# Order inside a step of seven matmul pairs: the dense lane's maximum product first, the other lane e m e m e e m

## The chip, the cores and the metric

The kernel runs on one NeuronCore of a Trainium2 chip. Its time is the device time of one execution in microseconds (us); lower is better. The engines that matter here are TensorE (PE in the profile; its weight loads are PEld), VectorE (DVE), ScalarE (ACT), GpSimd (POOL) and SyncE (SP), which issues the DMAs.

## The reference

A layernorm of x (2048 tokens of width 512) feeds two branches: attention with 32 query heads of width 16 that share one key and one value head, and a dense layer of width 1792 with Mish. The second gates the first.

```python
x = A_x
xn = _layernorm(x, axis=-1)
# A: q = xn @ wq in 32 heads, k = xn @ wk, v = xn @ wv
scores = jnp.einsum("bhqd,bkd->bhqk", q, k) * (Dh ** -0.5)
p = _softmax(scores, axis=-1)
o = jnp.einsum("bhqk,bkd->bhqd", p, v)
s = o.transpose(0, 2, 1, 3).reshape(B, S, H * Dh) @ wo
# B: h = xn @ w1 + b1, act = h * tanh(softplus(h))
g = _silu(act @ w2)
return x + s * g
```

Inputs and outputs are float32. The matmuls of this kernel split each operand into a high and a low part and add three products.

## The kernel before

The attention runs over 32 blocks (4 chunks of 512 queries, 8 groups of 4 heads in each), and a block is 16 steps. `s` counts the steps, and a step treats 2 x 2 score tiles. In one step TensorE makes, for the main part of the kernel:

- four **e** products (`e_one`): scores, keys on the partitions, 128 x 512. ScalarE turns each into its exponential `pt` (line L910). They use three PSUM banks in turn.
- four **m** products (`m_one`): scores of a later block, queries on the partitions, of which VectorE takes the row maximum (line L932). They too have three PSUM banks. From these maxima `c_rows` makes the shift rows of a block (lines L951 to L961, once per block), on VectorE as well.
- four **pv** products: values times the exponentials of two steps before. The trace shows each as two matmuls, so eight.
- six, seven, eight or no **x** products: halves of the other matmuls (q projection, dense layers 1 and 2, output projection). Such a matmul group has 12 or 15 products, all into the one PSUM bank `xps`; its sum is then read out (evacuated) by ScalarE (`hb` of the first dense layer, `qf` of the queries, `y` of the second layer's first third) or by VectorE (later thirds, `y` line L745, and the gate).

The e, m and x products use 64 of the array's 128 rows each, so that two run at once, one in either half. A half is called a lane here. In step s the **dense lane** is s % 2: the x products run there. The **other lane** has the four e and n of the m products; the remaining 4 - n are the dense lane's. `m_sides` sets n from the number k of x products: n is 3 for six and seven of them, 4 for eight. With six, both lanes have seven products, and the step is seven pairs; I call it a six-step, and those with seven and eight x a seven-step and an eight-step. A group of 12 takes four six-steps: six products in one lane, the same six (other half of the rows) in the other lane, then again. A group of 15 takes two eight-steps and two seven-steps.

`waves` writes the pairs out, an x and then one product of the other lane, until both lists are empty. The order on all engines is the order in which the code is written; nothing is reordered by a scheduler. Three rules in `waves` matter:

- **The relay.** The two halves of a product add into one bank from different lanes. So the first x of a step waits for an instruction of the step before: the consumer (exponential or maximum) of the first product that the other lane gets once the step's x products are all issued.
- **The evacuation** is issued right behind the last x of a group (`finish`), ahead of whatever the code issues later on that engine.
- **The hold.** If VectorE evacuates, the maxima issued while only one x is left (`HOLD`) go behind the evacuation.

Before, the other lane's list is made from the pattern "MEMEMEME", in which an M is left out when there is none: with n = 3 it is m e m e m e e.

Of the kernel before, what the change touches and what calls it, by code (L numbers as in the profile page):

```python
# [43 lines left out]
STEP_US = 2.95  # L44
XMAX = 8
NPT = 14
EM = "MEMEMEME"
MLAG = 4
NHB = 4
NXR = 2  # L50
# [12 lines left out]
def m_need(v):  # L63

    return (34, 64)[v] if v < 2 else 32 * (v + 1)
# [53 lines left out]
def block_kernel(ctx: ExitStack, tc: tile.TileContext, x, wq, wk, wv, wo, w1, b1, w2, out):  # L119
# [349 lines left out]

    held = [None]  # L470
    evacs = [0]
    cur = {"g": None, "ps": None, "n": 0, "chunk": [], "relay": None}

    def is_ready(g):
        return (all(i.tile is not None and i.ready <= step[0] for i in g.items)
# [7 lines left out]
    def begin():  # L483
        prepare()
        if qqueue and is_ready(qqueue[0]):
            g = qqueue.popleft()
        elif queue and is_ready(queue[0]):
            g = queue.popleft()
        else:
            n = next((n for n, g in enumerate(queue) if g.wo is None), None)  # L490
            if not n or not is_ready(queue[n]) or queue[n].m1 is None:
                return False
            g = queue[n]
            del queue[n]
        if g.start:
            g.start()
        if g.alloc:
            ps = g.alloc()
        else:
            ps = ps_x.tile([P, 512], F32, tag="x", name="xps")  # L500
        cur.update(g=g, n=0, ps=ps, chunk=[], relay=None)
        return True

    def finish():
        g = cur["g"]
        if cur["n"] < len(g.mms):
            return False
        for i in g.items:
            i.users -= 1
        cur["g"] = None  # L510
        evacs[0] += g.dve
        if lead:
            lead["post"](g, cur["ps"])
        else:
            g.post(cur["ps"])
            g.done = step[0]
        return True
# [14 lines left out]
    def chunk_size(n):  # L532
        return -(-n // -(-n // XMAX)) if n else 0

    def waves(h, em, new):

        if not cur["chunk"] and (not new or cur["g"] is None and not begin()):  # L540
            mms = []
        else:
            g = cur["g"]
            mms = cur["chunk"] or g.mms[cur["n"]:cur["n"] + chunk_size(len(g.mms) - cur["n"])]
        second = bool(cur["chunk"])
        k = len(mms)
        ms = em(k)
        a = deque(ms[1 - h])
        b = deque(ms[h])
        ps = cur["ps"]  # L550
        ends = second and cur["n"] + k == len(cur["g"].mms)
        xs = deque(mms)
        relay = None
        first = True
        done = False
        while a or b or xs:
            if xs:
                i = xs.popleft().half(ps, h)
                if first and cur["relay"] is not None:
                    tc.add_manual_dep(i.ins, cur["relay"].ins.name, mybir.DependencyInfo(  # L560
                        mybir.DependencyClass.Sync, mybir.DependencyReason.DATA), reason="other half of the bank")
                first = False
                if ends and cur["g"].dve and len(xs) == HOLD:
                    held[0] = []
                if not xs and ends:
                    cur["n"] += k
                    cur["chunk"] = []
                    finish()
                    done = True
                    for top in held[0] or ():  # L570
                        top()
                    held[0] = None
            elif b:
                b.popleft()()
            if len(a) > 1 or a and not xs:
                r = a.popleft()()
                if k and not xs and relay is None:
                    relay = r
        if k and not done:
            assert relay is not None  # L580
            cur["relay"] = relay
            if second:
                cur["n"] += k
                cur["chunk"] = []
            else:
                cur["chunk"] = mms
# [310 lines left out]
    def e_one(s, i):  # L897

        v, r = divmod(s, 16)
        if s < NS - LEAD:  # L900
            a, k, p = 1 - s % 2, r - r % 2 + i // 2, i % 2
        else:
            a, k, p = i % 2, r, i // 2
        q = qt_of[v]
        o = 64 * a
        ps, tag = (ps_m, "m") if NS - LEAD <= s and i in ((1, 3) if s < NS - 4 else (3,)) else (ps_e, "e")
        e = ps.tile([P, C], F32, tag=tag, name=f"e{s}_{i}")
        pe.matmul(e, ks[o:o + 64, P * k:P * (k + 1)], q[o:o + 64, p], start=True, stop=True)  # L908
        pt = sb.tile([P, C], F32, tag="pt", name=f"pt{s}_{i}", bufs=NPT)
        r = act.activation(pt, e, AF.Exp, scale=0.25)  # L910
        pt_of[16 * v + k, p, a] = pt
        return r
# [24 lines left out]
    def m_sides(h, n):  # L937

        ahead = m_next[h] - m_next[1 - h]
        lo = max((4 - MLAG - ahead + 1) // 2, 4 - (32 * NU - m_next[1 - h]))  # L940
        hi = min((4 + MLAG - ahead) // 2, 32 * NU - m_next[h])
        return max(min(n, hi), lo)
# [116 lines left out]
    def due(t):  # L1059
        step[0] = t  # L1060
        for k in sorted(k for k in timed if k <= t):
            for fn in timed.pop(k):
                fn()
# [84 lines left out]
    for c0, c1 in ((0, 1), (1, 2), (2, 3), (3, 4)):  # L1148
# [4 lines left out]
        for c in range(c0, c1):  # L1153
            xs, scs = [], []
# [65 lines left out]
    def best(eng):  # L1220
        found = None
        for k in plan[eng]:
            s = k.start(T[eng])
            if s is not None:
                rank = max(s, T[eng] + 0.1) + WAIT_US * k.prio
                if found is None or rank < found[2]:
                    found = (s, k, rank)
        return found
# [5 lines left out]
    while True:  # L1234
# [7 lines left out]
        b = best("PE")  # L1242
# [13 lines left out]
        s, e, k = min(opts, key=lambda o: o[0])  # L1256
# [34 lines left out]
        elif k == "J":  # L1291
            tag = next((g for g in ("wq", "ws", "wb") if (g == "wq" or s > 19.0) and arrived(g) and busy[0] + E0 < s + 0.5), None)
            n = ran[0]
# [16 lines left out]
    while left:  # L1310
        k = next(k for k in left if all(d.end is not None for d in k.deps))
# [10 lines left out]
    def pv_to(s):  # L1322

        while pv_next[0] <= s:
            k = pv_next[0]
            pv(k)
            pv_next[0] += 1
            if k % 16 == 15:
                o_out(k // 16)
                return  # L1330

    for s in range(NS + 2000):
        inm = s < NS - LEAD
        if inm or cur["chunk"]:
            assert s < NS
            due(s)
            h = s % 2

            def em(k):
                n = m_sides(1 - h, k // 2) if inm else 0  # L1340
                x = deque(lambda i=i: e_one(s, i) for i in range(4))
                y = deque(lambda: m_one(1 - h) for _ in range(n))
                r = [[], []]
                for op in EM:
                    if op == "M" and y:
                        r[1 - h].append(y.popleft())
                    elif op == "E":
                        r[1 - h].append(x.popleft())
                r[h] = [lambda: m_one(h) for _ in range(4 - n if inm else 0)]
                return r  # L1350

            if s >= 2 and (s - 1) % 16 == 0 and s > 1:
                gap[0] += 1
            waves(h, em, inm)
            act_jobs(1 + (len(jobs) > 2))
            due(s + 0.5)
            pv_to(s - 2)
            last = s + 1
        elif s < NS:
            if s == last and (NS - s) % 2:  # L1360
                for k in range(4):
                    e_one(s, k)
                due(s)
                fill(4)
                act_jobs(1)
                pv_to(s - 2)
            elif (NS - s) % 2 == 0:
                for k in range(6):
                    e_one(s + k // 4, k % 4)
                due(s)  # L1370
                fill(4)
                act_jobs(1)
            else:
                for k in range(2, 4):
                    e_one(s, k)
                due(s)
                fill(4)
                act_jobs(2)
                pv_to(s - 1)
        else:  # L1380
            due(s)
            act_jobs(100)
            pv_to(NS - 1)
            due(s + 0.5)
            fill(16)
        step[0] = s
        if vdone[0] < 8 * NC and min(m_next) >= m_need(vdone[0]):
            r = c_rows(vdone[0])
            rowq.extend([r[0], lambda r=r: (r[1](), r[2](), r[3]())])
            vdone[0] += 1  # L1390
        if rowq and not evacs[0]:
            rowq.popleft()()
        evacs[0] = 0
        pump()
        if s > NS + 1 and not queue and cur["g"] is None and not timed and not jobs:
            break
# [12 lines left out]
```

## Time and profile before

| | before |
|---|---|
| time, median of 3 runs | 1607.55 us (1606.56 to 1608.75) |
| span of the profiled execution | 1607.2 us |
| TensorE matmul busy | 1590.6 us (99%) |
| TensorE weight loads busy | 847.8 us (53%) |
| VectorE busy | 1344.9 us (84%) |
| ScalarE busy | 1298.3 us (81%) |
| GpSimd busy | 625.4 us (39%) |

The profiled execution's time is its span; the median of the runs is 0.3 us above it. TensorE's share is the time in which any matmul is under way, and since matmuls overlap and their ends are modelled, 99% doesn't mean that it could do no more.

### The profile page before, as it was taken

Reading aid. Unit: us, or ns where it says so; the run is one execution under the profiler, and the core shown is the slowest. Engines: PE = TensorE matmul, PEld = TensorE weight load, DVE = VectorE, ACT = ScalarE, POOL = GpSimd, SP = SyncE. Lnnn points to the kernel's source line nnn. Section 1 sums busy time; section 2 is a strip of 40 time slices with the busy share of each in tenths; the row PEclk is TensorE's granted clock in tenths of the full one; section 3 lists DMA queues with packets and bytes.
Section 4 is the critical chain, followed back from the end, with each engine's and each line's share of the span. In section 5 each row is a group of like instructions: output and inputs, shape, how many; then the busy total and the mean of one; then the engine's idle time right before and its main releaser. Section 6 shows DMA issues by size and latency. Waiting matters only on the chain.

```text
span 1607.2 us, 31497 instructions
## 1 busy us (share of the span) xinstructions
PE 1590.6 (99%) x11611; PEld 847.8 (53%) x11611; DVE 1344.9 (84%) x2299; ACT 1298.3 (81%) x2512; POOL 625.4 (39%) x640
## 2 busy tenths in 40 slices
PE   9999999999999999999999999999999999999998
PEld 5445555555555555555555555555555555555544
DVE  8898888888888888888898988888888888888812
ACT  7478788688898778978988787787798878779885
POOL 3276278066355103612514322172152323315522
PEclk9899999999999999999999999999999999999999
DMA  6233133142321304212103231221331223022020
GB/s 192 72 116 96 51 108 115 29 149 83 101 90 38 111 16 140 64 48 88 39 24 109 64 116 44 87 71 35 96 109 58 83 61 97 24 96 70 8 86 27
DMA packets 73001, 125.08 MB, mean 78 GB/s; under 512 B 21520, under 2 KB 33808, under 8 KB 72848
## 3 DMA queue, kind: packets, MB, share of 16 engines
q1 hardware_dynamic: 72848, 123.08, 24.4%
q8 instruction: 92, 1.51, 0.4%
q14 instruction: 61, 0.50, 0.1%
HBM read 75.57 MB, written 26.21 MB: 63 GB/s over the span
## 4 chain that ended last, share of the span: by engine, by line
PE 96%; DVE 1%; ACT 1%; POOL 0%; DMA 0%; SPq 0%; issue 0%; DVEq 0%; POOLq 0%
PE xps L112 43%; PE pv L982 32%; PE e L908 9%; PE m L928 8%; PE xps L108 3%; PE kp L312 1%; DVE mb L932 1%; PE wop L108 1%; ACT pt L910 0%; PE xp L280 0%; DMA xin<-in_dram 0%; DVE xt L156 0%; SPq L217 0%; ACT hb L671 0%; PE ol L1045 0%
## 5 line engine op out<-in xcount | busy, mean ns | idle before, releaser
L932 DVE TENSOR_REDUCE mb<-m 128x1 f32<-128x512 f32 x2048 | 1271.2, 682 | 184.2 <-PE m L928 149.0
L910 ACT ACTIVATE pt<-e 128x512 f32<-128x512 f32 x2048 | 1068.2, 605 | 250.9 <-PE e L908 240.9
L928 PE MATMUL m<-ks,qt 48*128 48x512 f32 (+1 forms) x2048 | 845.8, 424 | 4.2 <-DVE mb L932 2.9
L908 PE MATMUL e<-qt,ks 64*128 64x512 f32 x2048 | 746.7, 408 | 2.4 <-ACT pt L910 1.6
L982 PE MATMUL pv<-pt,vaug 128*32 128x512 f32 x4096 | 543.1, 604 | 0.0
L928 PEld LDWEIGHTS m<-ks,qt 48*128 48x128 f32 (+1 forms) x2048 | 373.1, 186 | 76.3 <-DVE mb L932 38.0
L908 PEld LDWEIGHTS e<-qt,ks 64*128 64x128 f32 x2048 | 372.4, 186 | 26.2 <-ACT pt L910 11.1
L112 PE MATMUL xps<-xt,ws 64*128 64x512 f32 x1266 | 351.2, 409 | 0.9 <-ACT pt L910 0.4
L112 PEld LDWEIGHTS xps<-xt,ws 64*128 64x128 f32 x1266 | 218.0, 185 | 204.8 <-ACT pt L910 137.7
L112 PE MATMUL xps<-wbs,act 64*128 64x512 f32 x1188 | 321.3, 407 | 0.0
L112 PEld LDWEIGHTS xps<-wbs,act 64*128 64x128 f32 x1188 | 207.0, 185 | 168.7 <-ACT pt L910 103.9
L166 POOL TENSOR_SCALAR t<-t 128x512 f32<-128x512 f32 x56 | 34.4, 614 | 323.8 <-ACT t L679 323.8
L982 PEld LDWEIGHTS pv<-pt,vaug 128*32 128x32 f32 x4096 | 81.9, 108 | 144.1 <-issue 135.8
L156 POOL TENSOR_TENSOR hb<-hb,t 128x512 f32<-128x512 f32 x56 | 72.2, 1289 | 116.1 <-ACT t L692 64.1
L112 PE MATMUL xps<-xt,wq 64*128 64x512 f32 x336 | 93.0, 409 | 0.0
L112 PEld LDWEIGHTS xps<-xt,wq 64*128 64x128 f32 x336 | 57.9, 185 | 54.1 <-ACT pt L910 35.2
L112 PE MATMUL xps<-wbs,ot_all 64*128 64x512 f32 x288 | 79.4, 408 | 0.0
L112 PEld LDWEIGHTS xps<-wbs,ot_all 64*128 64x128 f32 x288 | 49.5, 184 | 46.9 <-ACT pt L910 31.0
L156 POOL TENSOR_TENSOR hb<-hb,u 128x512 f32<-128x512 f32 x56 | 72.2, 1290 | 4.4
L156 POOL TENSOR_TENSOR u<-u,t 128x512 f32<-128x512 f32 x56 | 71.8, 1281 | 4.7
L156 POOL TENSOR_TENSOR act<-hb,act 128x512 fp32r<-128x512 f32 x55 | 70.7, 1286 | 4.6
L156 POOL TENSOR_TENSOR oc<-oc,sc 128x512 f32<-128x512 f32 (+1 forms) x16 | 20.6, 1287 | 121.3 <-ACT sc L1010 110.6
(121 smaller groups left out, 822.4 us busy)
## 6 DMA issues: line engine op xcount, KB each, us to landing
ws<-w SPq DMA_DIRECT2D x38, 512.0 KB
wbs<-w SPq DMA_DIRECT2D x36, 512.0 KB
qt<-qh SPq DMA_DIRECT2D x256, 32.0 KB
wq<-wq SPq DMA_DIRECT2D x14, 512.0 KB
w<-wbs SPq DMA_DIRECT2D x14, 512.0 KB
w<-ws SPq DMA_DIRECT2D x14, 512.0 KB
wbs<-wo SPq DMA_DIRECT2D x12, 512.0 KB
rawwb<-in_dram SPq DMA_DIRECT2D x20, 256.0 KB
```

Source lines behind the costliest of these rows:

```text
L108: self.pe.matmul(ps, self.lhs(), self.rhs(), start=(self.k == 0), stop=(self.k == self.tot - 1))
L112: i = self.pe.matmul(ps, self.lhs()[o], self.rhs()[o], start=(self.k == 0 and self.halves == 0), stop=(self.k == self.tot - 1 and self.hal ...
L156: eng.tensor_tensor(out=o, in0=a, in1=b, op=op)
L166: pool.tensor_scalar(o, o, lim, 0.0, op0=ALU.min, op1=ALU.max)
L312: pe.matmul(kp_of[c], wkf[:, dt], xf_of[c][dt // 2][:, dt % 2], start=(dt == 0), stop=(dt == 3))
L908: pe.matmul(e, ks[o:o + 64, P * k:P * (k + 1)], q[o:o + 64, p], start=True, stop=True)
L910: r = act.activation(pt, e, AF.Exp, scale=0.25)
L928: pe.matmul(m, q[o, p, P * t:P * (t + 1)], ks[o, C * kb:C * (kb + 1)], start=True, stop=True)
L932: return dve.reduce_max(out=mb_of[v][:, kb, z:z + 1], in_=m, axis=AX.X)
L982: pe.matmul(o[32 * j:32 * j + 32], vaug[:, k], pt, start=(k == 0), stop=(k == 15))
```

## The change

The pattern of the other lane depends on n: for three m it becomes e m e m e e m, for four it is as before. And in a step whose other lane has seven products (n is 3) the dense lane's one m is written before the first x, where before it stood behind the last.

```diff
-EM = "MEMEMEME"
+ORDERS = {3: "EMEMEEM", 4: "MEMEMEME"}
...
-    cur = {"g": None, "ps": None, "n": 0, "chunk": [], "relay": None}
+    cur = {"g": None, "ps": None, "n": 0, "chunk": [], "relay": None, "front": False}
...
         ms = em(k)
+        cur["front"] = k > 0 and len(ms[1 - h]) == 7
         a = deque(ms[1 - h])
         b = deque(ms[h])
...
         while a or b or xs:
-            if xs:
+            if xs and b and first and cur["front"]:
+                b.popleft()()
+                cur["front"] = False
+            elif xs:
                 i = xs.popleft().half(ps, h)
...
-                for op in EM:
+                for op in ORDERS.get(n, "MEMEMEME"):
```

The rows below are instructions in program order, with what each waits for in brackets (DVE and Activation are VectorE and ScalarE). First TensorE, the first five products of the step that ends one group of the first dense layer (its x products read `ws`); before:

```order
L112 MATMUL xps<-xt_1811,ws_9147 128x512 [waits Activation_49]
L928 MATMUL m_1_15_9657<-ks,qt_78 128x512 [waits DVE_49]
L112 MATMUL xps<-xt_1811,ws_9147 128x512
L908 MATMUL e_0_9661<-qt_77,ks 128x512
L112 MATMUL xps<-xt_1811,ws_9147 128x512
```

and with the change:

```order
L932 MATMUL m_0_17_9656<-ks,qt_78 128x512 [waits DVE_49]
L912 MATMUL e_0_9659<-qt_77,ks 128x512 [waits Activation_49]
L112 MATMUL xps<-xt_1811,ws_9147 128x512 [waits DVE_49]
L932 MATMUL m_1_15_9664<-ks,qt_78 128x512
L112 MATMUL xps<-xt_1811,ws_9147 128x512
```

The first e moves from the second pair to the first, and the first x from the first pair to the second; that x, the one with the relay, now waits for VectorE and not for ScalarE. The last five products of the same step on TensorE; before:

```order
L928 MATMUL m_1_17_9675<-ks,qt_78 128x512 [waits DVE_49]
L112 MATMUL xps<-xt_1811,ws_9147 128x512
L908 MATMUL e_2_9681<-qt_77,ks 128x512 [waits Activation_49]
L928 MATMUL m_0_17_9685<-ks,qt_78 128x512 [waits DVE_49]
L908 MATMUL e_3_9688<-qt_77,ks 128x512 [waits Activation_49]
```

and with the change:

```order
L912 MATMUL e_2_9677<-qt_77,ks 128x512 [waits Activation_49]
L112 MATMUL xps<-xt_1811,ws_9147 128x512
L912 MATMUL e_3_9682<-qt_77,ks 128x512 [waits Activation_49]
L112 MATMUL xps<-xt_1811,ws_9147 128x512
L932 MATMUL m_1_17_9689<-ks,qt_78 128x512 [waits DVE_49]
```

The fourth e moves from the seventh pair to the sixth, the last x from the sixth to the seventh, and an m is last. ScalarE in this step and at the start of the next; before:

```order
L910 ACTIVATE pt_0_9663<-e_0_9661 128x512 [waits PE_49]
L910 ACTIVATE pt_1_9672<-e_1_9670 128x512 [waits PE_49]
L671 ACTIVATE hb_10_9679<-xps,b1c 128x512 [waits PE_49]
L910 ACTIVATE pt_2_9683<-e_2_9681 128x512 [waits PE_49]
L910 ACTIVATE pt_3_9690<-e_3_9688 128x512 [waits PE_49]
L910 ACTIVATE pt_0_9709<-e_0_9707 128x512 [waits PE_49]
```

and with the change:

```order
L914 ACTIVATE pt_0_9661<-e_0_9659 128x512 [waits PE_49]
L914 ACTIVATE pt_1_9670<-e_1_9668 128x512 [waits PE_49]
L914 ACTIVATE pt_2_9679<-e_2_9677 128x512 [waits PE_49]
L914 ACTIVATE pt_3_9684<-e_3_9682 128x512 [waits PE_49]
L675 ACTIVATE hb_10_9687<-xps,b1c 128x512 [waits PE_49]
L914 ACTIVATE pt_0_9707<-e_0_9705 128x512 [waits PE_49]
```

The evacuation `hb` moves from behind the second exponential to behind the fourth. Of the 512 first exponentials (`pt_0`) of the steps, 236 have a second wait, for ScalarE itself, in the program before, and 34 with the change; of the third ones 77 and 121.

## Rows read from the trace of the kernel before

**Rows 1.** The page: busy time of each engine; the ending chain by line.

```profile
PE 1590.6 (99%) x11611; PEld 847.8 (53%) x11611; DVE 1344.9 (84%) x2299; ACT 1298.3 (81%) x2512; POOL 625.4 (39%) x640
...
PE xps L112 43%; PE pv L982 32%; PE e L908 9%; PE m L928 8%; PE xps L108 3%; PE kp L312 1%; DVE mb L932 1%; PE wop L108 1%; ACT pt L910 0%; PE xp L280 0%; DMA xin<-in_dram 0%; DVE xt L156 0%; SPq L217 0%; ACT hb L671 0%; PE ol L1045 0%
```

**Rows 2.** Groups by line and shape: count | busy us, mean ns | idle before.

```profile
L932 DVE TENSOR_REDUCE mb<-m 128x1 f32<-128x512 f32 x2048 | 1271.2, 682 | 184.2 <-PE m L928 149.0 <-PE xps L112 32.0 <-PE e L908 1.9
L910 ACT ACTIVATE pt<-e 128x512 f32<-128x512 f32 x2048 | 1068.2, 605 | 250.9 <-PE e L908 240.9 <-PE xps L112 3.8 <-PE m L928 1.7
...
L671 ACT ACTIVATE hb<-xps,b1c 128x512 f32<-128x512 f32 x56 | 38.7, 691 | 9.1 <-PE xps L108 9.1
...
L745 DVE TENSOR_TENSOR y<-xps,y 128x512 f32<-128x512 f32 x32 | 21.8, 682 | 51.2 <-PE xps L108 42.9 <-POOL qt L156 8.3
```

**Rows 3.** Busy time by stretch, 318.42 to 550.04: PE, PEld, DVE, ACT, POOL, PEclk.

```profile
318.42:550.04 231.62, 231.62 (x1761) 123.68 (x1761) 205.59 (x349) 197.23 (x380) 114.21 (x116) 1.00 0.30 94
```

**Rows 4.** Timeline of PE, PEld and ACT, six-step from 802.18: start us, us.

```profile
802.18 0.50 PE L112 MATMUL xps<-wbs,act 64*128 64x512 f32 x1
802.52 0.40 PE L908 MATMUL e<-qt,ks 64*128 64x512 f32 x1
803.68 0.49 PE L908 MATMUL e<-qt,ks 64*128 64x512 f32 x1
804.10 1.07 PE L982 MATMUL pv<-pt,vaug 128*32 128x512 f32 x8
805.09 0.50 PE L112 MATMUL xps<-wbs,act 64*128 64x512 f32 x1
...
803.67 0.18 PEld L908 LDWEIGHTS e<-qt,ks 64*128 64x128 f32 x1
...
803.01 2.06 ACT L910 ACTIVATE pt<-e 128x512 f32<-128x512 f32 x4 [0.33 <-PE e L908]
```

**Rows 5.** Timeline of PE, PEld and ACT, six-step from 810.87.

```profile
810.87 0.50 PE L112 MATMUL xps<-wbs,act 64*128 64x512 f32 x1
...
812.29 0.18 PEld L908 LDWEIGHTS e<-qt,ks 64*128 64x128 f32 x1
812.72 0.16 PEld L982 LDWEIGHTS pv<-pt,vaug 128*32 128x32 f32 x8 [0.24 <-issue]
...
811.64 1.57 ACT L910 ACTIVATE pt<-e 128x512 f32<-128x512 f32 x3 [0.27 <-PE e L908]
```

**Rows 6.** Timeline of PE, ACT and DVE, step without x from 98.70.

```profile
98.70 0.49 PE L928 MATMUL m<-ks,qt 64*128 64x512 f32 x1
...
99.27 2.06 ACT L910 ACTIVATE pt<-e 128x512 f32<-128x512 f32 x4
101.19 0.74 ACT L688 ACTIVATE t<-u,two 128x512 f32<-128x512 f32 x1
...
99.23 2.48 DVE L932 TENSOR_REDUCE mb<-m 128x1 f32<-128x512 f32 x4 [0.22 <-PE e L908]
```

**Rows 7.** Timeline of PE, seven-step from 992.35 and the next step's start.

```profile
992.35 0.50 PE L112 MATMUL xps<-wbs,act 64*128 64x512 f32 x1
...
994.09 0.39 PE L928 MATMUL m<-ks,qt 48*128 48x512 f32 x1
994.40 1.07 PE L982 MATMUL pv<-pt,vaug 128*32 128x512 f32 x8
995.40 0.50 PE L112 MATMUL xps<-wbs,act 64*128 64x512 f32 x1
```

**Rows 8.** Timeline of PE, DVE and PEld, six-step behind `c_rows`, from 500.55.

```profile
500.55 0.50 PE L112 MATMUL xps<-wbs,ot_all 64*128 64x512 f32 x1
...
500.86 0.19 DVE L956 TENSOR_REDUCE mp<-mp 128x16 f32<-128x32 f32 x1
...
501.39 1.25 DVE L932 TENSOR_REDUCE mb<-m 128x1 f32<-128x512 f32 x2
...
502.10 0.18 PEld L928 LDWEIGHTS m<-ks,qt 48*128 48x128 f32 x1 [0.31 <-DVE mb L932]
```

## The prediction

> **What bounds the kernel now.** I read the page first: TensorE has a matmul in flight 99% of the span and the chain that ended last runs almost wholly through its lines [rows 1], while VectorE's maxima and ScalarE's exponentials are 84% and 81% busy [rows 1, 2]. A busy TensorE is not a TensorE at its peak, so I went to the timeline of single steps, engine by engine. All times below are microseconds from the first product of a step.
>
> A six-step (six half products x, four e, four m) is one of 360 such steps that I count in the trace; 60 steps have seven x and 60 have eight. Take the one that starts at 802.18 [rows 4]. The products come in pairs, one on each half of the array: the first at 0, the second at 0.34 (802.52), then one every 0.23, so that the seventh stands at 1.50 (803.68). The four e go to pairs 2, 4, 6 and 7. The fourth e takes the PSUM bank of the first e (three banks). The exponential of the first e starts at 0.83 and lasts 0.60 [rows 2, 4]: done at 1.43. The weights of the fourth e are loaded at 1.49 (803.67), 0.06 later, and the pv products begin 0.43 after that load, at 1.92; the next step begins 0.99 after them, at 2.91. In the step at 810.87 the first exponential starts at 0.77 instead, the load comes at 1.42, pv at 1.85: again 0.43 after the load [rows 5]. So in both steps the end is set not by the slots but by one chain: first e, its exponential, the bank, fourth e, pv. The two starts differ because the program gives 236 of the 512 first exponentials a second wait, which costs them 0.06; the step at 810.87 has none.
>
> Without that wait pv could begin some 0.33 behind the seventh pair at 1.505, at 1.84, and a step would last 2.835: in a seven-step, whose last product is an m that waits for nothing, it is 0.31 (994.09 to 994.40 [rows 7]), and the seventh pair has an e a little behind the m. The mean is more: the stretch from 318.42 to 550.04 is 80 six-steps in a row, 231.62 / 80 = 2.895 [rows 3]. There is 0.06 per step to be had, 21.6 in all, and no more while the clock is at 1.00, its upper level of 2.4 GHz, as it is there.
>
> The Trainium skill, page "Perfetto Trace Analysis", section "Identifying the Most-Contended Engine", would judge TensorE by the busy share of its weight loads, not of its matmuls. By that share, 53% [rows 1], TensorE has room and VectorE is the most contended; a step would end no sooner than VectorE's four maxima of 0.60, at 2.4, and not at 2.835. The pairs at 0.23 in rows 4 speak against it: seven pairs and pv alone fill 2.835.
>
> **The change part by part.** No instruction is added or taken away; work is reordered in the 360 six-steps and in the 60 seven-steps, on TensorE, ScalarE and VectorE; the queues of GpSimd and SyncE, and so all DMAs, keep their order.
>
> (1) The first e and the dense lane's m become pair 1. The trace has steps that begin so, those without any x: in the one at 98.70 the first exponential starts at 0.57, the first maximum at 0.53, and the ScalarE instruction behind the four exponentials at 2.49 (101.19) [rows 6]. In the new order the first exponential ends at 1.17 and the fourth e loads at 1.22. It now stands in pair 6 (1.27), not 7; as the matmul follows its load by 0.10 (0.43 less the 0.33 above), it runs at 1.32, 0.05 late. One m follows in its lane, 0.23 later, at 1.55, and pv at 1.88; the step lasts 2.87. So the e that comes 0.34 earlier gives back 0.23 by standing one pair earlier. The gain is 2.895 - 2.87 = 0.025, times 360: **-9.0**. Of the first exponentials 34 keep a second wait in the new program: 34 x 0.06 = **+2.0**.
>
> In a seven-step the m of the other lane stands two pairs behind the fourth e, so nothing is pushed: 3.05 as before [rows 7].
>
> (2) A twelve-product group ends in a six-step, and its sum must leave the single xps bank before the next group's first x. Before, the evacuation stood behind the second exponential and was done long before it was needed. Now the last x is pair 7, and on ScalarE's queue, which runs in order, the evacuation stands behind all four exponentials: it starts at 2.49 and, at 0.69 [rows 2], ends at 3.18. Load at 3.23; the next step began at 2.87, so that is 0.36 into it, and x runs at 0.46. Its slot is now pair 2, at 0.34: 0.12 late, of which the 0.05 that the fourth e is late anyway are free. 52 groups end with hb: 52 x 0.07 = **+3.6**. The 14 copies of q I take at 0.60, like the exponentials, which read a tile of the same size from PSUM: they end 0.09 earlier, and what is left is within the slack: nothing. The 16 copies of y, also at 0.60, end a seven-step at 3.09, load at 3.14; the x that follows is mostly pair 1 of an eight-step, which would begin at 3.05: 16 x 0.09 = **+1.4**.
>
> (3) VectorE's evacuations (y, 0.68 [rows 2]) stood third of five on its queue and now stand fourth: 0.53 + 3 x 0.60 + 0.68 = 3.01, load at 3.06, 0.19 into the next step: in time. But the last maximum then ends at 3.61, its bank is wanted by the next step's pair 4 (2.87 + 0.80) instead of pair 5, and that m runs at 3.76: 0.09 late, 0.045 beyond the slack. 29 six-steps stand behind such a one: **+1.3**.
>
> (4) The half products of a bank change lanes from step to step, and the first x of a step waits for one instruction of the step before, the relay. It was the third exponential, done at 2.4; it becomes the step's last maximum, done at 3.01 (four of them take 2.48 from 0.53 [rows 6]). Load at 3.06, 0.19 into the step; x runs at 0.29, its slot is 0.34. That is free, with 0.05 to spare and 0.05 more behind it. Queued behind this x is everything on TensorE. It isn't free when VectorE has worked on the shift rows (c_rows): there the first maximum starts at 0.84 (501.39 in the step of 500.55), m waits until 1.55 (502.10) and pv, 0.43 behind that load, until 1.98 [rows 8], before and after alike. Now the four maxima also end at 3.29, the relay comes at 3.34 and x at 0.48 of the next step, 0.14 late, 0.09 beyond the slack. Before, the mean of 2.895 has these steps in it; the 2.87 has not, so they are added in full: 24 six-steps x (1.98 - 1.88 + 0.09) = **+4.6**.
>
> The sum is -9.0 + 2.0 + 3.6 + 1.4 + 1.3 + 4.6 = +3.9 on the span of 1607.2, 1611.1. The median of the runs is 0.3 above that span, which is less than the terms can tell: **1611**.
>
> Bounds. The 0.10 from load to matmul is inferred. If a late x must wait until its weights are in (0.18 to 0.19 of load), the waits of (2), (3) and (4) cost 0.09 more each, 121 times: +11, 1622. If the m behind the fourth e isn't pushed, pv comes at 1.84 and all 21.6 are won, but the slack of 0.05 is gone too: hb 52 x 0.155, y 1.4, (3) 29 x 0.125, (4) 24 x 0.27, second waits 1: 20.6 back, 1606.
>
> **The rivals.**
> - *The reorder wins.* The last sentence with the second half going otherwise: the step shrinks to 2.835 and the late evacuations and relays don't bite because VectorE and ScalarE start earlier too. If half of those 20.6 is hidden, 1607.2 - 21.6 + 10.3 = 1596; it is faster than the bound once less than 18 of them remain. For it: the first exponential does come 0.26 earlier. Against it: hb at 3.18 is arithmetic on rows 2 and 6. The share of weight loads in the Trainium skill's page "Perfetto Trace Analysis", named above, would favour this one.
> - *The relay binds every step.* If the wait for the maximum ends 0.1 later than I have it, the 270 six-steps that begin with a relayed x and not a fresh bank lose what goes beyond the slack. From 0.10 on each further 0.05 costs 13; at 0.15 it is 1624.
> - *Nothing measurable.* Gain and costs of some 9 and 13 are of one size; an error of a third in either leaves the time within 3 of now.
>
> **How the numbers follow.** A measurement of this kernel tells about 0.2%, 3.2, from no change. My forecast, a loss of a few microseconds by late evacuations and relays that outweigh a small gain, has 0.38 with 0.04 of it too small to see; the relay in every step 0.12; nothing measurable 0.28; the reorder wins 0.22. So faster 0.22, same 0.32, slower 0.46. The value is the likeliest one's, 1611, whose own range is 1607 to 1616. The range 1599 to 1622 leaves out the better half of the winning case and the worse part of the relay.
>
> **What the profile of the changed kernel would show.** (1) First exponential at 0.57 of a six-step, fourth e loaded at 1.22, pv at 1.88; wrong if pv stands at 1.84 or the exponential later than 0.6. (2) hb behind four exponentials, from 2.49, and behind it a step whose second pair starts at 0.46 with an idle weight load that ScalarE ends. (3) After y on VectorE, pair 4 about 0.09 late. (4) A relay that costs nothing in ordinary steps, and a late pair 2 behind c_rows. The prediction fails above all if the second pair is late in ordinary steps, or if it is on time even behind hb.

## The result, and the profile after

The changed kernel takes 1615.28 us (median of 6 runs, 1612.98 to 1618.84), the kernel before on the same chip 1607.94 (6 runs, 1604.81 to 1608.75): a ratio of 1.0048, 95% interval 1.0035 to 1.0061. The change costs 7.3 us. The profiled execution after has a span of 1613.5, 6.3 more than that of before.

The page of the changed kernel: busy time, the ending chain by line, and two groups of weight loads.

```profile
PE 1594.0 (99%) x11611; PEld 848.0 (53%) x11611; DVE 1345.2 (83%) x2299; ACT 1304.0 (81%) x2512; POOL 625.5 (39%) x640
...
PE xps L112 35%; PE pv L986 30%; PE m L932 17%; PE e L912 7%; PE xps L108 3%; ACT pt L914 2%; PE kp L312 1%; DVE mb L936 1%; PE wop L108 1%; PE xp L280 0%; ACT y L743 0%; DMA xin<-in_dram 0%; ACT hb L675 0%; ACT qf L615 0%; DVE xt L156 0%
...
L932 PEld LDWEIGHTS m<-ks,qt 48*128 48x128 f32 (+1 forms) x2048 | 364.4, 185 | 390.8 <-DVE mb L936 373.5
...
L112 PEld LDWEIGHTS xps<-wbs,act 64*128 64x128 f32 x1188 | 213.0, 185 | 79.6 <-ACT pt L914 21.8
```

Busy times are those of [rows 1] within half a per cent: no work was added, so the shares tell nothing of the 7 us. In the chain, m has gone from 8% to 17% and x from 43% to 35%, since an m now leads and ends the step. The 373.5 us of idle weight loads put down to VectorE are not a wait for VectorE: they are the 0.84 at the head of nearly every step while the pv products run, and have their name from the semaphore that the leading m looks at.

An ordinary six-step after, in the timeline, from 815.56:

```profile
815.56 0.50 PE L932 MATMUL m<-ks,qt 48*128 48x512 f32 x1
815.75 0.18 PEld L112 LDWEIGHTS xps<-wbs,act 64*128 64x128 f32 x1
815.90 0.39 PE L112 MATMUL xps<-wbs,act 64*128 64x512 f32 x1
816.09 2.48 DVE L936 TENSOR_REDUCE mb<-m 128x1 f32<-128x512 f32 x4 [0.40 <-PE e L912]
816.13 2.06 ACT L914 ACTIVATE pt<-e 128x512 f32<-128x512 f32 x4 [0.29 <-PE e L912]
816.77 0.18 PEld L912 LDWEIGHTS e<-qt,ks 64*128 64x128 f32 x1
817.12 0.40 PE L932 MATMUL m<-ks,qt 48*128 48x512 f32 x1
817.44 1.06 PE L986 MATMUL pv<-pt,vaug 128*32 128x512 f32 x8
818.44 0.18 PEld L932 LDWEIGHTS m<-ks,qt 48*128 48x128 f32 x1 [0.84 <-DVE mb L936]
```

The relayed x loads at 0.19 and runs at 0.34, its slot. The first exponential starts at 0.57 instead of the 0.77 to 0.83 of [rows 4, 5], the fourth e loads at 1.21, the last m is pushed to 1.56, pv stands at 1.88 and the next step at 2.88.

The same 80 steps as in [rows 3], busy time by stretch (PE, PEld, DVE, ACT, POOL, PEclk), take 232.80 in place of 231.62, at the same granted clock of 1.00:

```profile
317.90:550.70 232.80, 232.80 (x1764) 123.55 (x1761) 205.62 (x349) 198.75 (x380) 113.86 (x115) 1.00 0.30 93
```

I measured every step in the two traces, from its first product to the next step's, and sorted them by what stands beside them (us; the last column is the change over all steps of the row). A step counts as one with `c_rows` when their last instruction, a transposition, starts in it. A step goes into the first row that fits, with the rows on "next step has eight x" ahead of the others:

```
steps                                                     count  before  after   in all
six, evacuated by ScalarE, next step has eight x             10   2.895  3.125    +2.3
seven, evacuated by ScalarE, next step has eight x           10   3.048  3.178    +1.3
six, behind an evacuation by ScalarE                         58   2.911  2.982    +4.1
six, behind an evacuation by VectorE                         29   2.885  2.920    +1.0
six, with c_rows at its start                                20   2.958  2.908    -1.0
six, behind such a step                                      13   2.880  2.975    +1.2
six, ordinary                                               230   2.888  2.887    -0.1
seven, the others                                            50   3.090  3.082    -0.4
eight                                                        60   3.087  3.098    +0.7
no x                                                          8   2.745  2.713    -0.3
```

That is +8.9, of which the first three rows, the late evacuations by ScalarE, are 7.7. The span rose by 6.3 only, because the first of these steps began at 90.58 in the execution after and at 93.15 in that of before. That start goes with the clock: in the windows of the two traces, before and then after, the third figure from the end is the granted clock of TensorE in the stretch ahead of it, 0.93 and 0.96.

```profile
0.00:93.15 93.15, 85.83 (x333) 47.25 (x333) 81.40 (x163) 53.28 (x116) 38.55 (x49) 0.93 0.38 121
0.00:90.58 90.58, 83.49 (x333) 46.24 (x334) 81.32 (x163) 53.21 (x116) 38.57 (x49) 0.96 0.39 125
```

Behind the last of these steps both traces have 76.8 to 76.9.

The cost of an evacuation can be seen in one place, the step that ends a group of the first dense layer, from 757.69, and the next one, in the timeline of the changed kernel:

```profile
757.69 0.50 PE L932 MATMUL m<-ks,qt 48*128 48x512 f32 x1
758.26 2.07 ACT L914 ACTIVATE pt<-e 128x512 f32<-128x512 f32 x4 [0.82 <-PE m L932]
760.19 0.71 ACT L675 ACTIVATE hb<-xps,b1c 128x512 f32<-128x512 f32 x1
760.58 0.49 PE L932 MATMUL m<-ks,qt 48*128 48x512 f32 x1
760.95 0.18 PEld L112 LDWEIGHTS xps<-xt,ws 64*128 64x128 f32 x1 [0.19 <-ACT hb L675]
761.29 0.39 PE L912 MATMUL e<-qt,ks 64*128 64x512 f32 x1
762.54 1.06 PE L986 MATMUL pv<-pt,vaug 128*32 128x512 f32 x8
763.54 0.49 PE L932 MATMUL m<-ks,qt 48*128 48x512 f32 x1
```

`hb` starts behind four exponentials, at 2.50, and ends at 3.21, 0.32 into the next step. x loads 0.05 later, at 0.37, and the step lasts 2.96: 0.08 more than an ordinary one.

An eight-step begins with the x itself, and there a late evacuation keeps the whole step back; by the way the steps are measured, the time falls to the step that made the sum, not to the one behind it. A seven-step evacuated by ScalarE, from 146.85, in the timeline of the changed kernel, and then the same step before, from 148.83:

```profile
148.91 1.06 PE L986 MATMUL pv<-pt,vaug 128*32 128x512 f32 x8
149.34 0.63 ACT L743 ACTIVATE y<-xps 128x512 f32<-128x512 f32 x1
150.03 0.18 PEld L112 LDWEIGHTS xps<-wbs,act 64*128 64x128 f32 x1 [0.96 <-ACT y L743]
```

```profile
150.89 1.07 PE L982 MATMUL pv<-pt,vaug 128*32 128x512 f32 x8
151.05 0.62 ACT L739 ACTIVATE y<-xps 128x512 f32<-128x512 f32 x1
151.88 0.18 PEld L112 LDWEIGHTS xps<-wbs,act 64*128 64x128 f32 x1 [0.84 <-ACT y L739]
```

`y` now ends at 149.97, x loads 0.06 later, 1.12 behind the start of pv in place of 0.99. All ten such seven-steps last 3.17 or more in place of 3.05; of the ten six-steps, seven last 3.17 to 3.35, each with x loaded 0.05 to 0.14 behind the evacuation's end.

### The profile page after: what moved, and what is told of

Same layout as the page of the kernel before. It is cut to its first block, busy times and chain, and to the rows that moved or that the text cites. A ratio compares the mean times of both kernels' runs of the same rounds, so it can differ in the third digit from the quotient of the medians.

```text
span 1613.5 us, 31287 instructions
## 1 busy us (share of the span) xinstructions
PE 1594.0 (99%) x11611; PEld 848.0 (53%) x11611; DVE 1345.2 (83%) x2299; ACT 1304.0 (81%) x2512; POOL 625.5 (39%) x640
## 4 chain that ended last, share of the span: by engine, by line
PE 94%; ACT 3%; DVE 1%; issue 0%; POOL 0%; DMA 0%; SPq 0%; DVEq 0%; ACTq 0%; POOLq 0%
PE xps L112 35%; PE pv L986 30%; PE m L932 17%; PE e L912 7%; PE xps L108 3%; ACT pt L914 2%; PE kp L312 1%; DVE mb L936 1%; PE wop L108 1%; PE xp L280 0%; ACT y L743 0%; DMA xin<-in_dram 0%; ACT hb L675 0%; ACT qf L615 0%; DVE xt L156 0%
## 5 line engine op out<-in xcount | busy, mean ns | idle before, releaser
L932 PE MATMUL m<-ks,qt 48*128 48x512 f32 (+1 forms) x2048 | 794.4, 428 | 4.7 <-DVE mb L936 3.4
L912 PE MATMUL e<-qt,ks 64*128 64x512 f32 x2048 | 780.0, 425 | 2.6 <-ACT pt L914 1.6
L932 PEld LDWEIGHTS m<-ks,qt 48*128 48x128 f32 (+1 forms) x2048 | 364.4, 185 | 390.8 <-DVE mb L936 373.5
L112 PE MATMUL xps<-xt,ws 64*128 64x512 f32 x1266 | 333.7, 396 | 0.8 <-ACT pt L914 0.4
L112 PE MATMUL xps<-wbs,act 64*128 64x512 f32 x1188 | 310.6, 398 | 2.4 <-ACT hb L675 1.0
L112 PEld LDWEIGHTS xps<-wbs,act 64*128 64x128 f32 x1188 | 213.0, 185 | 79.6 <-ACT pt L914 21.8
L112 PEld LDWEIGHTS xps<-xt,ws 64*128 64x128 f32 x1266 | 226.1, 185 | 34.6 <-ACT hb L675 4.7
L112 PE MATMUL xps<-xt,wq 64*128 64x512 f32 x336 | 88.4, 396 | 0.0
L112 PE MATMUL xps<-wbs,ot_all 64*128 64x512 f32 x288 | 75.1, 393 | 0.0
L749 DVE TENSOR_TENSOR y<-xps,y 128x512 f32<-128x512 f32 x32 | 21.9, 683 | 51.2 <-PE xps L108 42.9
```

Source lines behind the costliest of these rows:

```text
L112: i = self.pe.matmul(ps, self.lhs()[o], self.rhs()[o], start=(self.k == 0 and self.halves == 0), stop=(self.k == self.tot - 1 and self.hal ...
L749: dve.tensor_tensor(out=y, in0=ps, in1=y, op=ALU.add)
L932: pe.matmul(m, q[o, p, P * t:P * (t + 1)], ks[o, C * kb:C * (kb + 1)], start=True, stop=True)
```

## The experiments

The theory is that of the prediction: the reorder gains little, and evacuations issued last and a relay read from VectorE's last maximum take it back. Two more questions came from the steps: why the ordinary step gains nothing at all, and whether the second wait on the first exponential, not the order, is what the old order loses.

**The evacuation ahead of the fourth exponential.** The changed kernel; in a step that ends a group evacuated by ScalarE the fourth exponential is kept back until the evacuation is issued.

```diff
+                if ends and not cur["g"].dve and len(xs) == k - 5:
+                    late[0] = []
...
+                    for top in late[0] or ():
+                        top()
+                    late[0] = None
```

> The changed kernel, but in a step that ends a group evacuated by ScalarE the evacuation is issued ahead of the fourth exponential instead of behind it. Theory (the late evacuation is what costs): in the trace of the changed kernel the 58 six-steps behind a ScalarE evacuation last 2.98 against 2.88 for the others, and the eight-steps behind one 3.13 against 3.08. The evacuation now ends about 0.5 earlier, at 2.70, so the second pair of the next step is back at 0.34 and these steps fall to 2.88: 58 x 0.10 + 16 x 0.05 = 6.6 less than the changed kernel's 1615.3, that is 1609, about the kernel before (1607.9). Rival (the relay, the last maximum, is what costs; the evacuation only stands beside it): the steps behind an evacuation keep their 2.98 and the time stays at 1613 to 1616.

Measured: 1605.80 (12 runs) beside 1604.90 for the kernel before (19 runs, which also stand beside the next two experiments and the pattern alone), ratio 1.0009 (0.9993 to 1.0024). The loss is gone. The two steps that were shown above, in its timeline:

```profile
752.01 1.58 ACT L923 ACTIVATE pt<-e 128x512 f32<-128x512 f32 x3 [0.82 <-PE e L918]
753.46 0.70 ACT L681 ACTIVATE hb<-xps,b1c 128x512 f32<-128x512 f32 x1
754.03 0.62 ACT L923 ACTIVATE pt<-e 128x512 f32<-128x512 f32 x1
754.32 0.50 PE L942 MATMUL m<-ks,qt 48*128 48x512 f32 x1
754.42 0.19 PEld L112 LDWEIGHTS xps<-xt,ws 64*128 64x128 f32 x1
756.20 1.06 PE L996 MATMUL pv<-pt,vaug 128*32 128x512 f32 x8
757.20 0.50 PE L942 MATMUL m<-ks,qt 48*128 48x512 f32 x1
```

`hb` ends at 754.16, before the next step begins at 754.32, and that step lasts 2.88. The 58 steps behind an evacuation by ScalarE fall from 2.982 to 2.889, and the ten six-steps and ten seven-steps with such an evacuation ahead of an eight-step go back to 2.896 and 3.054. All steps together are 0.1 above those of before, so the late evacuation is the whole of what the change loses on balance; the small losses that stay (VectorE's evacuations +1.0, behind `c_rows` +1.7) are paid by small gains elsewhere. The rival, the relay as the cost, falls: the relay is unchanged here.

**The old order in the steps that end a group.** The changed kernel, with the old pattern and no leading m there.

```diff
-        ms = em(k)
-        cur["front"] = k > 0 and len(ms[1 - h]) == 7
+        ends = second and cur["n"] + k == len(cur["g"].mms)
+        ms = em(k, ends)
+        cur["front"] = k > 0 and len(ms[1 - h]) == 7 and not ends
...
-                for op in ORDERS.get(n, "MEMEMEME"):
+                for op in ("MEMEMEME" if ends else ORDERS.get(n, "MEMEMEME")):
```

> The changed kernel, but the steps that end a group (some 90 of the 420) keep the old order: m leads, no product ahead of the first x, the evacuation behind the second exponential. Theory: the cost of late evacuations is gone (58 x 0.10, some 6), but in such a step x is pair 1 again and it waits for the relay, which is the last maximum of the changed step before it: that comes at 3.06 where the step could begin at 2.88, so 0.18 is lost at each: 90 x 0.18 = 16. Sum 1615.3 - 6 + 16 = 1625. Rival (the relay is free wherever it stands, the evacuation alone costs): 1609.

Measured: 1628.86 (5 runs), ratio 1.0130 (1.0111 to 1.0150); 4 above the forecast, and far from the rival's 1609. Three of the five runs had a granted clock of 0.993 or 0.994 over the whole run; the two at 0.998 took 1624.19 and 1624.89. All steps together are 17.9 above those of before, where 17 were forecast. An ending step that begins with the relayed x, from 639.46, in its timeline:

```profile
637.53 1.88 DVE L936 TENSOR_REDUCE mb<-m 128x1 f32<-128x512 f32 x3
...
638.27 1.07 PE L986 MATMUL pv<-pt,vaug 128*32 128x512 f32 x8
639.46 0.18 PEld L112 LDWEIGHTS xps<-xt,ws 64*128 64x128 f32 x1 [1.03 <-DVE mb L936]
```

The last maximum ends at 639.41 and x loads 0.05 later, 1.19 behind the start of pv in place of 1.00: 0.19 lost, as worked out. So the relay does cost where x is the first product; the m in front of x is what hides it.

**The kernel before with one buffer more.** Nothing is reordered; `NPT`, the number of buffers for the exponentials' results, goes from 14 to 15. That changes which exponentials the program gives a second wait.

```diff
-NPT = 14
+NPT = 15
```

> The kernel before with nothing changed but a fifteenth buffer for the exponentials' results (NPT 14 to 15). Theory (the 0.06 that the old order loses is the second wait of the first exponential, not the order): the program then gives 6 of the first exponentials a second wait instead of 217, and 178 of the second ones, whose bank has slack. The first exponential starts at 0.77 in nearly all six-steps, pv at 1.85: some 150 six-steps go from 2.91 to 2.85. Sum -8 to -13: 1595 to 1600, faster than both kernels, without the reorder. Rival (a second wait costs nothing; the 0.06 has another cause, which moves along with these steps): 1607 to 1609.

Measured: 1599.39 (8 runs), ratio 0.9957 (0.9941 to 0.9973), faster than both kernels. The step of [rows 4] is here at 799.43, the stretch of [rows 3] from 318.95; timeline, then busy time by stretch:

```profile
799.43 0.50 PE L112 MATMUL xps<-wbs,act 64*128 64x512 f32 x1
...
800.21 2.10 ACT L910 ACTIVATE pt<-e 128x512 f32<-128x512 f32 x4 [0.26 <-PE e L908]
800.86 0.18 PEld L908 LDWEIGHTS e<-qt,ks 64*128 64x128 f32 x1
801.28 1.06 PE L982 MATMUL pv<-pt,vaug 128*32 128x512 f32 x8
802.27 0.49 PE L112 MATMUL xps<-wbs,act 64*128 64x512 f32 x1
```

```profile
318.95:548.81 229.86, 229.86 (x1761) 121.86 (x1762) 205.60 (x349) 198.46 (x380) 114.56 (x116) 1.00 0.31 95
```

The exponential starts at 0.78, the load of the fourth e at 1.43, pv at 1.85, the next step at 2.84, where [rows 4] has 0.83, 1.49, 1.92 and 2.91. The 80 steps take 229.86, a mean of 2.873, and the 230 ordinary six-steps 2.860 in place of 2.888. 6.3 of the 8.5 that all steps together gain are theirs.

The second wait itself has a row in the traces: the view by line lists, on ScalarE's sequencer (ACTq), an `EVENT_SEMAPHORE` instruction at the line of the exponentials (count, shortest, median and longest in ns, first and last start in us). Before, from 802 to 804.9 (the step of [rows 4]), and then with fifteen buffers, from 799.4 to 802.2 (the same step):

```profile
L910 ACTq EVENT_SEMAPHORE  x1: 17/17/17, 803.0 to 803.0; - x1
```

```profile
L910 ACTq EVENT_SEMAPHORE  x1: 17/17/17, 800.7 to 800.7; - x1
```

Before, it stands right ahead of the first exponential (803.01); with fifteen buffers it stands ahead of the second, behind the first one's start at 800.21. The step of [rows 5] has none. Over the trace of before, 162 of the 360 six-steps have the row ahead of their first exponential; that starts at a median of 0.836 and the step lasts 2.912. The other 198 have 0.777 and 2.851. With fifteen buffers none of the 360 has the row there, and the first exponential starts at 0.776. In all steps together the first exponentials with such a row are 236 before, as listed, and 1 with fifteen buffers; the 217 and 6 of the expectation are not borne out. The rival, another cause of the 0.06, is out.

**The changed kernel with the same buffer.**

> The changed kernel with the fifteenth buffer for the exponentials' results that made the kernel before 5 to 6 faster. Theory (the buffer only takes a second wait off the first exponential, and in the new order that exponential no longer ends the step): only 34 first exponentials have the second wait to lose, and the fourth e stands behind its slot as before; 34 x 0.06 = 2 at most, 1613 to 1616. Rival (the buffer helps by another way, as through the pv products' release of the buffers): 5 to 8 less, 1607 to 1610.

Measured: 1616.18 (8 runs) beside 1608.84 (13 runs), ratio 1.0052 (1.0033 to 1.0072), as the changed kernel without it. The buffer helps only where the first exponential ends the step, which fits the second wait and not another use of the buffer. The trace of the changed kernel has no such row ahead of a first exponential in any of its 360 six-steps, so there was nothing left to take away.

**The pattern alone.** No m is put ahead of x.

```diff
-        cur["front"] = k > 0 and len(ms[1 - h]) == 7
+        cur["front"] = False
```

> One half of the change: the pattern e m e m e e m of the other lane, but the dense lane begins with x as before, no m ahead of it. Theory: the dense lane's m then stands behind its six x instead of ahead of them, so the four maxima start later, with the second pair; the fourth m finds its bank free only at about 1.50 and runs at 1.60, pv at 1.93, a six-step lasts 2.92; evacuations stay early enough. 360 x 0.03 = 11 and the relay at pair 1 adds some: 1620 to 1632, slower than the whole change. Rival (the pattern is what costs and the m ahead of x is neutral): about 1615, as the whole change.

Measured: 1644.25 (4 runs), ratio 1.0226 (1.0202 to 1.0251). The direction is the theory's, the size is not: pv stands at 1.97 in the usual six-step, not at 1.93, and the mean six-step is 2.983: 360 x (2.983 - 2.895) = 32 and not 360 x 0.03. Why pv is 0.04 later than worked out stays open.

**The leading m alone.** The other lane keeps m e m e m e e.

```diff
-ORDERS = {3: "EMEMEEM", 4: "MEMEMEME"}
+ORDERS = {3: "MEMEMEME", 4: "MEMEMEME"}
```

> The other half of the change: the dense lane's m ahead of its first x, with the other lane in its old pattern m e m e m e e. Theory: two m stand in the first pair, so four m come in 1.04 and the fourth, in pair 5, wants the bank of the first maximum, which ends at about 1.3; it and all behind it in its lane (two e) move on by some 0.3, the fourth e and pv with them: six-steps of 3.15 to 3.2, 360 x 0.27 = 97, about 1700 to 1715. Rival (the m in front is neutral): 1605 to 1615.

Measured: 1715.42 beside 1607.77 (4 and 11 runs), ratio 1.0672 (1.0657 to 1.0687), six-steps of 3.17, as worked out. The time is at the upper edge of the forecast; the seven-steps, which it had left out, add 10.5. Each half alone is far worse than the whole: the leading m must not have another m beside it, and the pattern needs the m in front.

**One more small instruction on VectorE in each six- and seven-step,** in the changed kernel and in the kernel before: a maximum over 64 numbers, behind the first maximum, 422 in the trace.

```diff
+            r = dve.reduce_max(out=mb_of[v][:, kb, z:z + 1], in_=m, axis=AX.X)
+            if cnt[0] == 1:
+                more_dve()
+            return r
```

> The changed kernel with one small instruction more on VectorE behind the first maximum of each six- and seven-step (a maximum over 64 numbers per partition, by the nearest row, a reduction of 32 numbers in the shift rows, some 0.1 to 0.19; 420 of them). Theory (the relay, now the step's last maximum, is on time in ordinary steps with 0.05 to spare and 0.05 more behind it): the relay comes 0.10 to 0.19 later, x of the next step's second pair at 0.39 to 0.48 in place of 0.34, so what goes beyond the slack, 0.00 to 0.09, is lost in the some 240 six-steps that begin with a relayed x: 0 to 22; with 0.15 it is 12, 1627. Rival (the relay has far more room, or is not what x waits for): the time goes up by no more than that of the kernel before with the same instruction.

> The kernel before with the same instruction added in the same place. Here the relay is the third exponential on ScalarE, and VectorE's four maxima and the instruction (2.4 to 2.6) still fit into a step of 2.89; only the banks of the maxima come free later. Theory: under 8, at most 1615. Rival (VectorE bounds the step whatever the order, as its place as the busiest engine would have it): as much as in the changed kernel, 12 or more.

Measured: 1632.18 for the changed kernel (5 runs, ratio 1.0143, 1.0128 to 1.0158) and 1616.92 for the other (6 runs, 1.0057, 1.0042 to 1.0071), beside the same 1607.77. VectorE's timeline in the changed kernel with the instruction:

```profile
432.94 0.69 DVE L947 TENSOR_REDUCE mb<-m 128x1 f32<-128x512 f32 x1 [0.19 <-PE e L913]
433.55 0.21 DVE L928 TENSOR_REDUCE zz<-zz 128x1 f32<-128x64 f32 x1
433.67 1.88 DVE L947 TENSOR_REDUCE mb<-m 128x1 f32<-128x512 f32 x3
```

It lasts 0.21 but moves the next maximum by only 0.12 (433.55 to 433.67). By that, the relay is 0.12 late. The ordinary six-steps of the changed kernel grow by 0.030 (2.887 to 2.917), those of the kernel before not at all (2.888 and 2.887), and the steps behind an evacuation by VectorE by 0.085 and 0.082. So in the changed kernel 0.09 of the 0.12 disappear: the slack of 0.05 and 0.05 that the prediction had. The kernel before was 1.9 above the bound that I had set; it loses in the steps with `c_rows` (+2.5) and in those behind VectorE's evacuations (+2.4), which I had not counted. The Trainium skill, page "Perfetto Trace Analysis", section "Identifying the Most-Contended Engine", takes the engine with the highest occupancy as the bottleneck, with TensorE judged by MFU and by the busy share of its weight loads; by the latter, 53%, that is VectorE here. The two runs disagree: 422 x 0.12, some 50 us more on VectorE, cost the kernel before 9.

## Why the prediction was right, and where it was not

The sign was right, the main cause, evacuations issued last, was named, and the time, 1615.3, lies in the likeliest case's own range of 1607 to 1616. The loss itself was forecast at 3.9; it is 7.3 by the medians and 8.9 by the steps. That the span of the profiled execution rose by 6.3 only is chance: it began its main part 2.6 earlier, at a higher granted clock. By the prediction's steps:

- **(1) The reorder, -9.0 and +2.0.** The mechanism was right, to the times in the step: exponential at 0.57, load at 1.21 for 1.22, pv at 1.88, last m pushed to 1.56. The size was wrong: ordinary six-steps changed by -0.1 in all, not by some -4.5 (230 x 0.025 less their part of the second waits). The subtraction 2.895 - 2.87 failed, in both numbers. The 2.895 is a mean with the steps behind `c_rows` and evacuations in it; ordinary ones had 2.888. The 2.87 was added up from rows with two decimals; the median is 2.878, and with a few longer steps the mean is 2.887. What happened is this: in the old order an ordinary step lasted 2.849 (131 steps without the second wait) or 2.911 (99 with it, medians). The new order rids it of the second wait and puts the fourth e a pair earlier and an m behind it, and all steps last 2.88. Fifteen buffers show what it would be without either: 2.85. The second waits were put in the wrong steps, too. Of the 236 before, 162 stand in six-steps, so 162 x 0.06 = 9.7 was to be had there and not 21.6; of the 34 that stay all are in eight-steps, and the +2.0 is nothing.
- **(2) The late evacuation, +3.6 and +1.4.** Right, undone by one edit, and larger than forecast: 7.7. The 43 six-steps behind `hb` went from 2.912 to 3.012, +4.3 in all; against ordinary steps of the same trace that is 0.12 each, 5.2, where 52 x 0.07 = 3.6 was forecast. The instants were right (`hb` at 2.50 to 3.21 for 2.49 to 3.18, x loaded at 0.37 for 0.36; the pair behind x stands at 0.71, 0.14 late where 0.12 was worked out), the slack taken off was too large, and some are later than the one shown (median 2.981, the longest 3.16). Six more `hb` stand ahead of an eight-step, where x has no pair in front of it; they add 1.3. The copies of q cost nothing where a six-step follows, as forecast (nine, 2.911 before and after), but the four ahead of an eight-step cost 1.0. The 16 copies of y cost 1.3, as forecast at 1.4: all of it at the ten that stand ahead of an eight-step (`y` ends at 3.12 and x loads at 3.18, for 3.09 and 3.14), while behind the other six a six-step is in time (2.876).
- **(3) VectorE's evacuation, +1.3.** Measured +1.0.
- **(4) The relay, +4.6.** Free in ordinary steps, as said: x loads at 0.19 and runs in its slot, and 0.12 of added delay shows 0.03 of itself. Behind `c_rows` the second pair was late as said; 13 such steps lost 1.2, and ten more, which stand behind an evacuation too, changed by 1.0 in all. The rest of the 4.6, 24 x 0.10, was the step of `c_rows` itself, which came into the sum only to mend the mean of 2.895 and was taken as equal before and after; it is 0.05 shorter after (2.958 and 2.908), -1.0 in all.

Seven-steps without a late `y`, costed at nothing, changed by -0.4. Of the rivals, "the reorder wins" is excluded by the first experiment: even with the evacuations in time the new order only equals the old one (1605.80 and 1604.90). "The relay binds every step" is excluded by x at 0.34. "Nothing measurable" was near: the ordinary step is unchanged; what makes the loss measurable is (2).

What stays open: why a second wait whose own row lasts 17 ns puts the exponential off by 60 ns, and why the slack behind `hb` was smaller than worked out.

## What to carry to other kernels

Cost a reorder by the chain that ends the step, and take both sides of the difference from steps of one kind: a mean over a stretch has the disturbed steps in it. When a loss is counted by steps, look where a late first product shows: in the step before it. When an accumulation's last product moves to the end of a step, look at what the evacuation now stands behind on its in-order engine; issuing it one instruction earlier gave back all that the reorder lost. When a step comes in two lengths, ask which semaphore waits differ before reordering: here one buffer more gained what the reorder was after, without moving an instruction.

## What the runs showed of the hardware

- A wait more on an instruction is not free: the first exponential of a six-step starts 0.06 later with it (0.836 and 0.777, medians of 162 and 198 steps). The Trainium skill, page "Perfetto Trace Analysis", section "Identifying Dependency Chains", says that an instruction that waits for several engines may get semaphore instructions of its own put ahead of it. The trace agrees: the second wait is an `EVENT_SEMAPHORE` row of 17 ns at 803.0, right ahead of the exponential at 803.01, though here that wait is for ScalarE itself.
- A late product costs the pair behind it, too: x loads and is recorded at 760.95, and the next pair comes 0.34 later (761.29), like the second pair of any step, and not 0.23.
- A product that waits for an evacuation loads its weights 0.05 to 0.06 behind the evacuation's end (760.90 and 760.95; 149.97 and 150.03).
- A small instruction on VectorE lasts 0.21 in its row but costs 0.12 in the queue, since it starts before the one ahead has ended (432.94 and 0.69, 433.55).
- The start of the main part moved by 7.5 between the ten profiled executions (88.72 to 96.20), about as much as the whole change costs, and it goes with the granted clock ahead of it: 0.98 and 1.00 at the two earliest (88.72 and 89.08), 0.91 at 94.44, 0.89 at 96.20. In the trace of before the clock was at 0.50, the lower level of 1.2 GHz, from 50.9 to 57.7 and from 67.9 to 74.7; in the 5.9 and 5.1 us ahead of these TensorE had a matmul under way for 4.86 and 3.86. Of the runs at a granted clock of 0.999, the changed kernel took 1612.98 and 1613.32, the kernel before 1603.32 to 1605.03 (four runs beside the first experiment): the difference is nearer to the 8.9 of the steps than to the 7.3 of all runs.
